# The triangular solve of a chunked recurrence: the whole triangle in two banks of PSUM, and its inverses applied as 64x64 diagonal tiles

## The chip, the cores and the metric

The kernel runs on one core of a Trainium2 chip. It has five engines with a queue each: TensorE (PE in the profile; its weight loads are PEld), VectorE (DVE), ScalarE (ACT), GpSimd (POOL) and SyncE (SP, which issues DMAs here). TensorE writes its results to PSUM, eight banks of 128 x 512 fp32 words; everything else lies in SBUF or in device memory. Each engine works its own queue in order and waits on semaphores. The metric is the device time of one launch in microseconds (us); less is better.

## The reference, cut to what matters

The kernel computes a recurrent attention (a state of 40 x 40 for each of 4 x 8 batch-heads, over 768 steps) and a mixture of experts behind it:

```python
for t in range(S):                       # S = 768, D = 40, B*H = 32
    y[:, :, t] = einsum('bhd,bhde->bhe', rt, state)
    Sa = einsum('bhde,bhe->bhd', state, at)
    state = state * wt[:, :, None, :] - einsum('bhd,bhe->bhde', Sa, bt) \
            + einsum('bhd,bhe->bhde', vt, kt)
x = y as [B*S, H*D]                      # 3072 tokens of 320
# experts: tokens with x @ w_skip > 0 go to the expert of their largest
# logit (8 experts, 320 -> 1024 -> 320, relu), scaled by the softmax weight
# of that logit, and are added to x; the others pass through.
```

All of it is fp32. What matters here is the attention. Because each step removes `Sa` (which depends on the state) and adds it back along `b`, 32 steps at once form a triangular system: with N the strictly triangular 32 x 32 matrix of products of `a` and `b` inside a chunk, the chunk needs the inverse of (1 - N), applied to what the old state and the chunk's own `k`, `v` give.

## The kernel before, in words

The 768 steps are cut into 24 chunks of 32, and `attn` walks them in one Python loop, `for c in range(NC)`. Four chunks make a group `ph` (six groups), and 64 steps make a half-group `h`. The two halves of the heads, `x` = 0 and 1, run as two interleaved recurrences. For each chunk and each `x` the path of the recurrence is: `ux` (16 matmuls against `L1`, one for each of 16 batch-heads, into PSUM, then one ScalarE copy to `UXs`), `uq` (the chunk's inverse applied to `UXs`, then four ScalarE copies into `R1t`, and a mask on POOL), `sst` (the new state, again through PSUM and ScalarE or VectorE), and for every second chunk `rs` (the state scaled back by VectorE). Beside that path run `m1` (the products that make N, one pair of calls for each `h` and `x`), `kbt` and `wtt` (transposes on TensorE), `m2` (products of `v` and `r`), `yy` (the output, one VectorE multiply `XS` for each chunk, and two DMAs out), scans on VectorE (`scan_z`, `scan_w`), products on POOL (`kbm`, `l1a`) and the routing of finished tokens to the experts (`m.route`, many small VectorE operations, and an indirect DMA).

The inverses come from `tinv(ph)`, for one group at a time, while the chunks of the group before it run. There are 128 systems (4 chunks x 32 batch-heads) and each lies in one partition, so the solve is only VectorE. It is a forward substitution by columns: step j multiplies column j of N by row j of the inverse found so far (an outer product of (31-j) x k elements, into a scratch tile `tmp_`), and subtracts that from the rows below. The columns of the inverse are split in two blocks that go side by side, so that the pair of operations of one block stands between the pair of the other. The first `SPL` = 8 columns (`X0`) lie in a PSUM bank (`px`), the other 24 columns (`Xi`) in SBUF, in the big tile `M`. In the profile the first block's operations read `M<-M,px` (product) and `px<-px,M` (subtraction). Those of the second block read `M<-M` for both. 30 steps in the first block and 22 in the second make 104 VectorE operations for each of the five solves (groups 1 to 5; group 0 has a solve of its own, `tinv0`). At the end ScalarE copies `X0` to `Xi`, and one VectorE transpose writes the inverses to `TB`, where `uq` reads them as weights: four matmuls of 32 x 32 for each `hh`, one for each block of 32 partitions.

Two things set the order of the work. The first two chunks and the last two stand in the order in which the code calls them. From chunk 2 up to chunk 22 the calls are only recorded by `Rec`, which then places them (`flush`, `plan`): a list scheduler with estimated costs for each operation, which decides the order on all five engines and which bank of PSUM each tile gets. In the profile the recorded instructions carry L209 and the others L109. The planner may use the banks of `pq`, `pc` and `ps`, two of each, so six; `py` (one bank, for `yy`) and `px` (one bank, for `X0`) are not its own. Outside the plan `m1`, `kbt`, `wtt`, `m2`, `s1`, `s2` and the routing take their tiles from the ring `ps_p`, which from the end of the prologue on is the two banks `pq`. The planner is told which POOL and VectorE operations depend on each other, but its costs know nothing of one engine slowing another.

## Time and profile before

| | us |
|---|---|
| median of three runs | 662.9 (660.15 to 670.07) |
| the profiled execution | 660.01 |
| its span in the profile | 658.2 |
| VectorE busy | 519.6 (79%) |
| TensorE busy | 507.4 (77%) |
| ScalarE busy | 423.6 (64%) |
| POOL busy | 321.6 (49%) |

The span is cut into stages below: the prologue and chunk 0 (0 to 89 us), chunk 1 (to 110.2), chunks 2 and 3 (to 152.2), then four chunks in each of the next stages (to 231.2, 311.6, 391.8 and 454.6), the end of the recurrence and the last routing (to about 507), and the experts (to 658). A row of the groups' view gives line, engine, operation, tiles written and read, one shape, the count, then busy us and mean ns of one, then the idle time of the engine before them. Shapes are written partitions x elements. A row of the timeline gives start and duration in us, then engine, line, operation and tiles. A matmul of fp32 is recorded as two instructions, so 16 calls read x32.

### The profile page before, as it was taken

To read this page: it belongs to the slowest core of one execution; us is meant where nothing else is said; L and a number is where in the kernel's file an instruction comes from. 1 tells how busy PE (TensorE), PEld (TensorE's weight loads), DVE (VectorE), ACT (ScalarE), POOL (GpSimd) and SP (SyncE) were. 2 spreads that over 40 slices of the span, in tenths; PEclk is the share of its full clock that TensorE was granted. 3 is DMA by queue.
4 is the path that set the end of the run, shared out by engine and by line. 5 is a ranking of instruction groups with operands and counts; after the bars stand their busy time and mean duration, and the time that the engine had idled before them with its cause. 6 is when DMAs were issued, how large, how long until landed. Compare 5 with 4: busy or idle time off the path is not lost. (4 is left out here: it accounts for less than half of the span.)

```text
span 658.2 us, 30327 instructions
## 1 busy us (share of the span) xinstructions
PE 507.4 (77%) x13236; PEld 424.8 (65%) x13236; DVE 519.6 (79%) x1182; ACT 423.6 (64%) x1103; POOL 321.6 (49%) x256
## 2 busy tenths in 40 slices
PE   5766676687588778858758578888678799999994
PEld 2544465566476657637547466767566599899994
DVE  7998778988989789997998977884274458888871
ACT  6463565587766867757768578898966155455540
POOL 5491952645536665375733634333131156566661
PEclk9697778779877986888969799999977799999998
DMA  7784566352444525345334243454535166667200
GB/s 183 215 229 153 133 181 218 114 150 86 124 119 132 162 74 142 107 130 161 102 106 121 82 129 101 133 168 119 156 99 146 57 193 207 214 216 233 81 25 24
DMA packets 67817, 90.85 MB, mean 138 GB/s; under 512 B 32756, under 2 KB 54849, under 8 KB 66190
## 3 DMA queue, kind: packets, MB, share of 16 engines
q1 hardware_dynamic: 62638, 74.31, 39.0%
q0 software_dynamic: 5040, 14.54, 6.8%
q8 instruction: 106, 1.74, 1.1%
q14 instruction: 33, 0.27, 0.1%
HBM read 74.03 MB, written 17.08 MB: 138 GB/s over the span
## 5 line engine op out<-in xcount | busy, mean ns | idle before, releaser
L209 DVE TENSOR_TENSOR M<-M 128x130 f32<-128x130 f32 (+10 forms) x202 | 106.2, 526 | 2.2
L209 ACT COPY R1t<-pq 32x416 f32<-32x416 f32 (+4 forms) x218 | 84.1, 386 | 31.7 <-PE pq L209 28.7
L209 POOL TENSOR_TENSOR R1t<-R1t,mc 64x512 f32<-64x512 f32 x40 | 53.8, 1346 | 86.3 <-ACT R1t L209 62.8
L109 POOL TENSOR_TENSOR WL<-WR,WH 128x1280 fp32r<-128x1280 f32 (+1 forms) x21 | 57.6, 2779 | 8.7 <-ACT WH L109 8.6
L209 ACT COPY R1t<-pc 32x128 f32<-32x128 f32 (+4 forms) x146 | 53.3, 365 | 9.7 <-PE pc L209 7.7
L209 PE MATMUL py<-L2t,R1t 128*32 128x40 f32 x1280 | 22.9, 220 | 27.4 <-DVE XS L209 14.4
L209 POOL TENSOR_TENSOR WR<-WR,M 128x1024 f32<-128x1024 f32 x14 | 33.7, 2422 | 14.9 <-DMA WR<-kb 14.6
L109 ACT CAST WH<-WR 128x1024 fp32r<-128x1024 f32 (+1 forms) x35 | 39.6, 1132 | 0.0
L209 DVE TENSOR_TENSOR px<-px,M 128x168 f32<-128x168 f32 (+8 forms) x141 | 37.1, 263 | 3.1
L209 PEld LDWEIGHTS py<-L2t,R1t 128*32 128x32 f32 x1280 | 18.1, 124 | 31.9 <-issue 16.9
L109 DVE CAST ti<-xe 128x2 int32<-128x2 f32 x8 | 38.0, 4747 | 0.2
L109 POOL DMA_INDIRECT out<-ro,ti x16 | 15.7, 982 | 45.7 <-PE pq L109 21.8
L109 ACT ACTIVATE hH<-pc 128x512 fp32r<-128x512 f32 x21 | 12.6, 598 | 38.3 <-PE pc L109 38.3
L209 POOL DMA_INDIRECT xg<-XS,ix x20 | 24.6, 1232 | 25.1 <-DVE M L209 11.1
L209 DVE TENSOR_TENSOR M<-M,px 128x168 f32<-128x168 f32 (+8 forms) x141 | 34.7, 246 | 1.3
L209 DVE TENSOR_TENSOR_SCAN M<-M 128x1041 f32<-128x1041 f32 (+1 forms) x14 | 32.5, 2320 | 0.2
L209 POOL TENSOR_TENSOR M<-M,mc 128x256 f32<-128x256 f32 x16 | 12.1, 756 | 41.6 <-issue 25.4
L109 PE MATMUL pc<-xH,WH 128*128 128x256 f32 x126 | 32.4, 282 | 0.0
L109 DVE TENSOR_TENSOR WL<-WR,WH 128x1024 fp32r<-128x1024 f32 (+1 forms) x19 | 23.8, 1253 | 8.4 <-ACT WH L109 7.8
L209 DVE TENSOR_TENSOR R1t<-pc,D 40x512 f32<-40x512 f32 (+1 forms) x32 | 19.2, 601 | 13.3 <-PE pc L209 12.9
L209 PE MATMUL ps<-R1t,L2t 128*40 128x40 f32 (+1 forms) x512 | 26.3, 244 | 2.5 <-ACT R1t L209 1.1
L209 PE MATMUL pq<-UX,TB 32*32 32x72 f32 (+1 forms) x800 | 23.6, 262 | 5.5 <-ACT R1t L209 5.3
(380 smaller groups left out, 1692.9 us busy)
## 6 DMA issues: line engine op xcount, KB each, us to landing
WR<-kb SPq DMA_DIRECT2D x10, 1024.0 KB
WR<-w SPq DMA_DIRECT2D x16, 640.0 KB
WR<-w SPq DMA_DIRECT2D x16, 512.0 KB
vvt<-vv POOLq DMA_DIRECT2D x21, 256.0 KB, 4.1
rrt<-rr POOLq DMA_DIRECT2D x10, 512.0 KB, 5.6
M<-wt SPq DMA_DIRECT2D x9, 520.5 KB
M<-at SPq DMA_DIRECT2D x8, 512.0 KB
WR<-w SPq DMA_DIRECT2D x16, 256.0 KB
```

What stands on the lines that cost most here:

```text
L109: if not s.on: return fn(*a,**k)
L209: for fn,a,k,own in s.tasks[i].calls: fn(*[at(x,own) for x in a],**{n:at(x,own) for n,x in k.items()})
```

## The change

It does three things.

The second block of the solve moves from SBUF to PSUM. `SPL` becomes 12, so that the first block is 32 x 12 words (`X0`) and the rest of the triangle is 20 x 20 (`X1`), each in a bank of its own, and no operation of the solve proper has all its operands in SBUF any more. The second block now has 18 steps instead of 22, and a tile `X1` of 400 words is copied back by ScalarE beside `X0`.

The banks are dealt out anew: `px` gets two banks and `pq` one. The planner so has five banks instead of six, and the ring `ps_p` has one bank where the order is that of the code.

`uq` applies the inverses from chunk 4 on as 64 x 64 weights, with two 32 x 32 blocks on the diagonal and zeros beside them: two matmuls for each `hh` instead of four. For that the last transpose of the solve writes to `NL_` (in `M`), and eight DMAs on SP's queue set the blocks into three tiles `TBw`, two in `SCR` and one in `TB`, which three DMAs from a tensor of zeros have cleared (issued at chunks 2 and 5). The first group keeps the 32 x 32 form.

```diff
--- before.py
+++ after.py
@@ -221,7 +221,7 @@
         if len(shape)==2: return t
         ax=["abcd"[q] for q in range(len(shape)-1)]
         return t.rearrange("p ("+" ".join(ax)+") -> p "+" ".join(ax),**{a:v for a,v in zip(ax,shape[1:])})
-G2=1; TD=(1,3); BU0=6; BU=(2,0,0,0); BX=(0,0,0,0,0,1,0,0,0,0,2,2,1,1,1,0,0,0,1,2,0,1,1,1,1,0,1,0,0); SPL=8; SCAN_POOL=0; RN=192; RB=((),()); RLAST=(('0c','1b','3a','3c'),('0a','0c')); P2=0
+G2=1; TD=(1,3); BU0=6; BU=(2,0,0,0); BX=(0,0,0,0,0,1,0,0,0,0,2,2,1,1,1,0,0,0,1,2,0,1,1,1,1,0,1,0,0); SPL=12; SCAN_POOL=0; RN=192; RB=((),()); RLAST=(('0c','1b','3a','3c'),('0a','0c')); P2=0
 ROUTE=('0c',('0c','1b','3c'),('0c','1b','3c'))
 WT=(1,0,0,0,1)
 def attn(ctx,tc,i,m,out,X):
@@ -232,7 +232,7 @@
     cp=P("const",1).pool; wk=P("wk",1); wk2=P("wk2",2); wk3=P("wk3",3); wk4=P("wk4",4)
     pp=m.pp
     bk=lambda n,k: [pp.tile([128,512],F32,name=f"{n}{q}") for q in range(k)]
-    PQ,PC,PS,PY,PX=bk("pq",2),bk("pc",2),bk("ps",2),bk("py",1),bk("px",1)
+    PQ,PC,PS,PY,PX=bk("pq",1),bk("pc",2),bk("ps",2),bk("py",1),bk("px",2)
     rec.banks={t.name:t for t in PQ+PC+PS}; rec.rest=[t.name for t in PS]
     ps_c,ps_s,ps_p=(Ring(t,rec) for t in (PC,PS,PQ)); ps_y,ps_x=Ring(PY),Ring(PX); m.ps=ps_p
     V,A,G,TE,SP=nc.vector,nc.scalar,nc.gpsimd,nc.tensor,nc.sync
@@ -241,19 +241,22 @@
     NR1=2; NL=4; NL2=2; NTB=3
     mQ,idn=m.mQ,m.idn
     WR=m.WR
-    mp=tc.tile_pool(name="M",bufs=1,side="right"); M=mp.__enter__().tile([128,13300],F32,name="M")
+    mp=tc.tile_pool(name="M",bufs=1,side="right"); M=mp.__enter__().tile([128,13400],F32,name="M")
     off=[0]
     def mv(n):
         o=off[0]; off[0]+=n; return M[:,o:o+n]
     w_,Z_,rv,a_,AB_,NL_,X_,l3=(mv(n) for n in (1041,1042,1041,1024,1024,1024,1024,1024))
-    AT_=[mv(256) for _ in range(2)]; Wx_=[mv(1040).rearrange("p (a b) -> p a b",a=16) for _ in range(4)]; tmp_=[mv(192) for _ in range(2)]; an=[0]
+    AT_=[mv(256) for _ in range(2)]; Wx_=[mv(1040).rearrange("p (a b) -> p a b",a=16) for _ in range(4)]; tmp_=[mv(240) for _ in range(2)]; an=[0]
     sq=lambda t: t.rearrange("p (a b) -> p a b",a=32)
     KBa=[WR[:,2048*q:2048*q+2048].rearrange("p (u c q t) -> p u c q t",u=16,c=2,q=2) for q in range(4)]
     L1t=cp.tile([128,4096],F32,name="L1t")
     l1s=[[WR[:,8192:9216],WR[:,9216:10240],WR[:,10240:11264]]+[l3]+[L1t[:,1024*q:1024*q+1024] for q in range(4)]][0]
     L1=[[l1s[2*n+x].rearrange("p (u c t) -> p u c t",u=16,c=2) for n in range(NL)] for x in range(2)]
     TB=cp.tile([128,NTB*512],F32,name="TB"); SCR=cp.tile([128,2048],F32,name="SCR")
-    TBa=[TB[:,512*q:512*q+512].rearrange("p (h m) -> p h m",h=16) for q in range(NTB)]
+    TBn=[TB[:,o:o+512].rearrange("p (h m) -> p h m",h=16) for o in (1024,0)]
+    TBw=[t.rearrange("p (h m) -> p h m",h=16) for t in (SCR[:,0:1024],SCR[:,1024:2048],TB[:,0:1024])]
+    TBa=TBn
+    def tbw(h): return TBw[(h+1)%NTB]
     L2t=cp.tile([128,5120],F32,name="L2t"); R1t=cp.tile([128,5632],F32,name="R1t")
     L2=[[L2t[:,1280*(2*n+x):1280*(2*n+x)+1280].rearrange("p (c u d) -> p c u d",c=2,u=16) for n in range(NL2)] for x in range(2)]
     R1=[[R1t[:,3328*n+(1664,1152)[n]*x:][:,:(1664,1152)[n]].rearrange("p (u n) -> p u n",u=16) for n in range(NR1)] for x in range(2)]
@@ -391,28 +394,29 @@
         ab=AB[0]
         NLt=sq(NL_)
         V.transpose(NLt.rearrange("p a b -> p (a b)"),ab.rearrange("p a b -> p (a b)"))
-        Xi=sq(X_)
-        X0=ps_x.tile([128,32,SPL],F32)
+        Xi=sq(X_); K=32-SPL
+        X0=ps_x.tile([128,32,SPL],F32); X1=ps_x.tile([128,K,K],F32)
         V.tensor_tensor(X0,NLt[:,0:SPL].rearrange("p s t -> p t s"),m.mT[:,:,0:SPL],ALU.mult)
-        V.tensor_tensor(Xi[:,:,SPL:32],NLt[:,SPL:32].rearrange("p s t -> p t s"),m.mT[:,:,SPL:32],ALU.mult)
+        V.tensor_tensor(X1,NLt[:,SPL:32,SPL:32].rearrange("p s t -> p t s"),m.mT[:,SPL:32,SPL:32],ALU.mult)
         V.memset(X0.rearrange("p a b -> p (a b)")[:,0:SPL*SPL:SPL+1],-1.0)
-        V.memset(Xi.rearrange("p a b -> p (a b)")[:,33*SPL::33],-1.0)
+        V.memset(X1.rearrange("p a b -> p (a b)")[:,::K+1],-1.0)
         yield
         for i in range(1,31):
             q=[]
-            for g,(j,lo,hi,X) in enumerate(((i,0,min(i,SPL),X0),(i+SPL,SPL,i+SPL,Xi))):
+            for g,(j,o,X) in enumerate(((i,0,X0),(i+SPL,SPL,X1))):
                 if j>30: continue
-                n=31-j; k=hi-lo
-                tmp=tmp_[g]
-                tv=tmp[:,:n*k].rearrange("p (a b) -> p a b",b=k)
-                V.tensor_tensor(tv,NLt[:,j,j+1:32].unsqueeze(2).broadcast_to([128,n,k]),X[:,j,lo:hi].unsqueeze(1).broadcast_to([128,n,k]),ALU.mult)
-                q.append((tv,X[:,j+1:32,lo:hi]))
+                n=31-j; k=min(i,SPL) if g==0 else i
+                tv=tmp_[g][:,:n*k].rearrange("p (a b) -> p a b",b=k)
+                V.tensor_tensor(tv,NLt[:,j,j+1:32].unsqueeze(2).broadcast_to([128,n,k]),X[:,j-o,0:k].unsqueeze(1).broadcast_to([128,n,k]),ALU.mult)
+                q.append((tv,X[:,j+1-o:32-o,0:k]))
             for tv,xv in q: V.tensor_tensor(xv,xv,tv,ALU.subtract)
             yield
-        A.copy(Xi[:,:,0:SPL],X0)
-        s0=(2*ph)%NTB; s1=(2*ph+1)%NTB
-        t0=TBa[s0]; d=bass.AP(t0.tensor,t0.offset,(tuple(t0.ap[0]),(TBa[s1].offset-t0.offset,2),(32,16),(1,32)))
-        V.transpose(d.rearrange("p h (x f) m -> p m x h f",x=2),Xi)
+        A.copy(Xi[:,:,0:SPL],X0); A.copy(Xi[:,SPL:32,SPL:32],X1)
+        t0=NL_.rearrange("p (w h m) -> p w h m",w=2,h=16)
+        V.transpose(t0.rearrange("p w (x f) m -> p m x w f",x=2),Xi)
+        for w in range(2):
+            for b in range(4):
+                r=slice(32*b,32*b+32); SP.dma_start(tbw(2*ph+w)[r,:,32*(b%2):32*(b%2)+32],t0[r,w])
         yield
     def tinv0(Xi):
 
@@ -484,11 +488,11 @@
         UXd[x]=UXs
     def uq(c,x):
         if c<0: return
-        R=R1[x][c%NR1]; Tb=TBa[(c//2)%NTB]; uu=slice(uo[x],uo[x]+32); n=RW[c%2]
+        R=R1[x][c%NR1]; uu=slice(uo[x],uo[x]+32); n=RW[c%2]; k=32 if c<4 else 64; Tb=TBn[c//2] if c<4 else tbw(c//2)
         UQ=ps_c.tile([128,4,n],F32,tag="pc",name="psUQ")
         for hh in range(4):
-            for b in range(4):
-                q=slice(32*b,32*b+32)
+            for b in range(128//k):
+                q=slice(k*b,k*b+k)
                 TE.matmul(UQ[q,hh,:],Tb[q,x*8+hh*2+c%2,:],UXd[x][q,hh,0:n],start=True,stop=True)
         for b in range(4):
             A.copy(R[uu,4*b:4*b+4,:],UQ[32*b:32*b+32,:,:])
@@ -720,7 +724,10 @@
             if c: rs(c,1)
             else: warm(BX[8])
             if c==1: s2(1,0,(0,0,1,1))
-            if c==2: s2(1,1,(0,0,1,1))
+            if c==2:
+                s2(1,1,(0,0,1,1))
+                for q in range(2): SP.dma_start(SCR[:,1024*q:1024*q+1024],i['zer'][:,0:1024])
+            if c==5: SP.dma_start(TB[:,0:1024],i['zer'][:,0:1024])
             T()
             if j==1: kbt(2*ph+1,2)
             if j==3: kbt(2*ph+2,2)
@@ -764,7 +771,7 @@
         next(ra)
         yy(NC-1,1)
         run_all(ra)
-        m.pr=[Ring.of(ps_c.t+ps_x.t),Ring.of(ps_s.t+ps_y.t),ps_p]
+        m.pr=[Ring.of(PC+PX[:1]),Ring.of(PS+PX[1:]),Ring.of(PQ+PY)]
         p2=[m.pr[0].tile([128,512],F32) for _ in range(2)]; pt=[p2[0][:,0:256],p2[0][:,256:512],p2[1][:,0:256]]
         rb=m.route(xl[:,1:2],1,NC-1,lambda: onehot(1))
         warm(WT[1]); m.xacc(pt,0)
```

On VectorE, where the solve of the third group (`ph` = 2) begins, the order before is:

```order
L209 STREAM_TRANSPOSE M<-M 128x1024
L209 TENSOR_TENSOR px_106<-M,mc 128x256
L209 TENSOR_TENSOR M<-M,mc 128x32x24
L209 TENSOR_TENSOR M<-M,px_106 128x30
L209 TENSOR_TENSOR px_106<-px_106,M 128x30
L209 TENSOR_TENSOR M<-M,px_106 128x58
L209 TENSOR_TENSOR px_106<-px_106,M 128x29x2
L209 TENSOR_TENSOR M<-M 128x22
L209 TENSOR_TENSOR M<-M,px_106 128x84
L209 TENSOR_TENSOR M<-M 128x22
```

The same place in the changed program, with operations of the recurrence (`R1t`) between:

```order
L209 STREAM_TRANSPOSE M<-M 128x1024
L209 TENSOR_TENSOR px_105<-M,mc 128x384
L209 TENSOR_TENSOR R1t<-ps_102,D_511 40x8x40 x2
L209 TENSOR_TENSOR px_106<-M,mc 128x400
L209 MEMSET px_105 128x12
L209 MEMSET px_106 128x20
L209 TENSOR_TENSOR M<-M,px_105 128x30
L209 TENSOR_TENSOR M<-M,px_106 128x18
L209 TENSOR_TENSOR px_105<-px_105,M 128x30
L209 TENSOR_TENSOR px_106<-px_106,M 128x18
```

Each operation of the second block now names a bank, `px_106`, and the triangle's mask is applied into two banks (384 and 400 elements) instead of one bank and `M` (256 and 768).

On TensorE, in chunk 1, where the tiles come from the ring in the order of the code, the order before is (`WR,L1t` are the two calls of `m1`, `mc,WE` is `wtt`, `mc,WR` is `kbt`):

```order
L109 MATMUL pq_99<-WR,L1t 32x64 x16
L109 MATMUL pq_100<-WR,L1t 32x64 x16
L109 MATMUL pq_99<-mc,WE_456 128x104 x4
L109 MATMUL pq_100<-mc,WR 128x104 x4
L109 MATMUL ps_103<-mc 128x512
```

and in the changed program:

```order
L109 MATMUL pq_99<-WR,L1t 32x64 x32
L109 MATMUL pq_99<-mc,WE_456 128x104 x4
L109 MATMUL pq_99<-mc,WR 128x104 x4
L109 MATMUL ps_102<-mc 128x512
```

The four tiles that went to two banks in turn now go to one bank, one behind the other.

On SP, where the inverses of the group `ph` = 3 are set in place in the changed program (`R1t<-vt` is `load_v`, `WR<-M` the DMAs of `m1`), with nothing of the kind before:

```order
L209 DMA WR<-M 32x256 x4
L209 DMA WR<-zer 32x1024
L209 DMA R1t<-vt 32x16x40
L209 DMA SCR<-M 32x16x32 x4
L209 DMA TB<-M 32x16x32 x4
L209 DMA M<-zer 32x1024
L209 DMA WR<-M 32x256 x4
L209 DMA M<-at 128x1024
```

Eight DMAs stand on SP's queue ahead of the next loads.

## The prediction

> **What bounds the kernel now.** The page's chain of waits reaches back only to 506 us, into the expert phase, which this change leaves alone. So I read the recurrence by stages. The timeline of TensorE gives the first matmul with new inverses (`uq` of chunks 4, 8, 12, 16 and 20), and so the stages' bounds:
>
> ```profile
> 152.17 0.92 PE L209 MATMUL pq<-UX,TB 32*32 32x104 f32 x32
> 231.21 0.92 PE L209 MATMUL pq<-UX,TB 32*32 32x104 f32 x32
> 311.58 1.11 PE L209 MATMUL pq<-UX,TB 32*32 32x104 f32 x32
> 391.80 0.92 PE L209 MATMUL pc<-UX,TB 32*32 32x104 f32 x32
> 454.59 1.28 PE L209 MATMUL pc<-UX,TB 32*32 32x104 f32 x32
> ```
>
> Busy time by stage (from:to, length; then busy us of PE, PEld, DVE, ACT and POOL with instruction counts; granted clock, DMA share, GB/s):
>
> ```profile
> 89.00:110.20 21.20, 14.77 (x527) 12.38 (x524) 17.27 (x65) 14.92 (x42) 5.25 (x4) 0.83 0.68 203
> 110.20:152.20 42.00, 31.23 (x1089) 26.75 (x1087) 36.56 (x92) 28.06 (x81) 21.27 (x22) 0.80 0.38 115
> 152.20:231.20 79.00, 58.87 (x1986) 48.32 (x1980) 71.50 (x185) 58.27 (x168) 42.14 (x38) 0.85 0.43 125
> 231.20:311.60 80.40, 60.07 (x1995) 50.34 (x1984) 71.54 (x185) 58.48 (x168) 45.55 (x38) 0.81 0.42 124
> 311.60:391.80 80.20, 55.18 (x1983) 45.68 (x1977) 73.48 (x180) 56.24 (x162) 41.94 (x34) 0.87 0.39 110
> 391.80:454.60 62.80, 52.68 (x1860) 42.66 (x1853) 47.56 (x177) 55.51 (x159) 21.39 (x22) 0.97 0.46 130
> ```
>
> In the three stages of about 80 us DVE is busy 89 to 92%, ACT and PE some 70 to 75%. The fourth runs the same recurrence and the same kind of solve in 62.8 us, with POOL at 21 instead of 42 us. So VectorE sets the pace from 152 to 392, and the groups of its time say why. First all solves, then the second block (`M<-M`) in each of the four stages:
>
> ```profile
> L209 DVE TENSOR_TENSOR M<-M 128x130 f32<-128x130 f32 (+10 forms) x202 | 106.2, 526 | 2.2
> L109 DVE TENSOR_TENSOR M<-M 128x42 f32<-128x42 f32 (+7 forms) x16 | 5.6, 353 | 0.0
> ...
> L209 DVE TENSOR_TENSOR M<-M 128x22 f32<-128x22 f32 (+10 forms) x44 | 26.7, 607 | 0.5
> ...
> L209 DVE TENSOR_TENSOR M<-M 128x22 f32<-128x22 f32 (+10 forms) x44 | 26.4, 600 | 0.5
> ...
> L209 DVE TENSOR_TENSOR M<-M 128x22 f32<-128x22 f32 (+10 forms) x44 | 28.6, 651 | 0.5
> ...
> L209 DVE TENSOR_TENSOR M<-M 128x22 f32<-128x22 f32 (+10 forms) x44 | 14.4, 328 | 0.4
> ```
>
> The same 44 operations take 26 to 29 us where POOL works much, and 14.4 where it works little. The timelines of DVE and POOL show it happen:
>
> ```profile
> 205.71 2.20 DVE L209 TENSOR_TENSOR M<-M 128x42 f32<-128x42 f32 x1
> 208.15 0.23 DVE L209 TENSOR_TENSOR px<-px,M 128x56 f32<-128x56 f32 x1
> 208.28 3.08 DVE L209 TENSOR_TENSOR M<-M 128x22 f32<-128x22 f32 x1
> ...
> 205.69 2.15 POOL L209 TENSOR_TENSOR WR<-WR,M 128x1024 f32<-128x1024 f32 x1
> 209.17 2.15 POOL L209 TENSOR_TENSOR WR<-WR,M 128x1024 f32<-128x1024 f32 x1
> ```
>
> A product of 42 elements begins with a POOL operation (205.69 to 207.84) and ends with it at 207.91. The one of 22 ends at 211.36, with the POOL operation that ends at 211.32. Between them an operation with a bank of PSUM among its operands took 0.23 us. VectorE's operations with all operands in SBUF wait for POOL's; those with PSUM don't.
>
> **The solve on VectorE.** The second block's 18 steps do sum i(19-i) = 1140 elements, each in a product and a subtraction. Prices come from the shapes of the first block:
>
> ```profile
> L209 DVE TENSOR_TENSOR px<-px,M 128x184 f32<-128x184 f32 x4 | 1.4, 354 | 0.1
> L209 DVE TENSOR_TENSOR px<-px,M 128x8 f32<-128x8 f32 x5 | 0.9, 174 | 0.2
> L209 DVE TENSOR_TENSOR M<-M,px 128x184 f32<-128x184 f32 x4 | 1.4, 344 | 0.1
> L209 DVE TENSOR_TENSOR M<-M,px 128x8 f32<-128x8 f32 x5 | 0.8, 163 | 0.2
> L109 DVE TENSOR_TENSOR M<-M 128x60 f32<-128x60 f32 x2 | 0.4, 212 | 0.0
> ...
> L209 DVE TENSOR_TENSOR M<-M,mc 128x768 f32<-128x768 f32 x4 | 6.0, 1498 | 0.0
> ...
> L209 DVE TENSOR_TENSOR px<-M,mc 128x256 f32<-128x256 f32 x4 | 3.3, 827 | 0.1
> ```
>
> That is 166 ns + 1.02 an element for a subtraction, 155 + 1.03 for a product. 18 x 0.321 + 1140 x 0.00205 = 8.1 us a solve. The first block grows from 8 to 12 columns, so by 2024 - 1140 = 884 elements (2024 is the old second block): 884 x 0.00205 = 1.8 us. Masks: 0.83 + 1.50 before; two of about 1.0 by the same rows (1.31 ns an element between them) after, so 0.3 less. The last transpose I leave at its 2.0. A solve loses its second block and gains 9.9 - 0.3 = 9.6: the four stages lose 17.1, 16.8, 19.0 and 4.8 us of DVE. The first solve had 106.2 + 5.6 - 26.7 - 26.4 - 28.6 - 14.4 = 15.7 and loses 6.1.
>
> The Trainium skill (VectorE: DVE Perf Modes, "The TRN2 errata") speaks against this. It gives an operation from PSUM a fixed 120 cycles and one from SBUF 58, at 0.96 GHz, so an estimate by that page makes each of the 36 operations of the second block 65 ns dearer than in SBUF, 2.3 us a solve. No such price shows here: `M<-M` of 60 elements, undisturbed in the fifth row, took 212 ns, and the two lines above give 217 and 227 for 60. The sum stays with the rows.
>
> **What is late next.** With 17 us less, DVE would be at 55 of 80 us. The stage from 391.8 shows how full others can be when VectorE doesn't bind: ACT 55.51/62.8 = 88%, PE 52.68/62.8 = 84%. ACT gains a copy of 400 elements and 128 more in the other one:
>
> ```profile
> L209 ACT COPY R1t<-pq 32x416 f32<-32x416 f32 x52 | 25.8, 496 | 5.9 <-PE pq L209 5.2
> ```
>
> About 0.5 + 0.1 us a solve. So the stages come out at the longer of PE/0.84 and (ACT + 0.6)/0.88: 70.1, 71.5 and 65.7 us, all by PE (ACT gives 66.9, 67.1, 64.6). Against 79.0, 80.4 and 80.2 that is 8.9 + 8.9 + 14.5 = 32 us. The fourth is already there: 0. Of the first solve most lies from 110.2 to 152.2 (DVE 87%); PE/0.84 gives 37.2, so at most 5 us, and I take 4.
>
> **The 64x64 tiles.** How long is `uq`?
>
> ```profile
> 217.80 0.79 PE L209 MATMUL ps<-R1t,L2t 128*40 128x40 f32 x32
> ...
> 219.01 0.70 PE L209 MATMUL pq<-UX,TB 32*32 32x72 f32 x32
> ...
> L209 PE MATMUL py<-L2t,R1t 128*32 128x40 f32 x1280 | 22.9, 220 | 27.4 <-DVE XS L209 14.4
> ```
>
> A single matmul's 220 ns is, by my estimate, all fill and drain. What is left of the 0.70, with four blocks at once and so 8 deep, is 0.48/8 = 60 ns for 72 columns, 0.83 ns a column. The row above, 40 wide and so two at once, is 16 deep: 0.57/16 = 36 ns for 40 columns, 0.89. Half the instructions, two at once, are again 8 deep: 0.7 us as before. The bounds are 0 and half of it for 40 `uq`, 14 us. I take 0.
>
> **The new DMAs** stand between the solve and its use. SP's own pace, a POOL-queue load's time to landing (the nearest row with one), and two last transposes:
>
> ```profile
> 217.69 2.62 SPq L209 DMA_DIRECT2D L1t<-M  x4
> ...
> vvt<-vv POOLq DMA_DIRECT2D x21, 256.0 KB, 4.1
> ...
> 220.32 1.98 DVE L209 STREAM_TRANSPOSE TB<-M 128x1024 f32<-128x1024 f32 x1
> ...
> 383.61 1.98 DVE L209 STREAM_TRANSPOSE TB<-M 128x1024 f32<-128x1024 f32 x1
> ```
>
> The first chunk needs four of the eight: 2.6 us to issue and up to 4.1 to land, 6.7. Between transpose and first use lay 231.21 - 222.30 = 8.9 us, and 391.80 - 385.59 = 6.2. A faster solve ends earlier, so I count 0; without that cover it is up to 5 x 6.7 = 34 us. The 5.2 us in which SP issues all eight delay the loads behind them (`at`, `v` of a later chunk, N's products), which are a chunk ahead, some 16 to 20 us. The 1.5 MB of zeros hide beside a DMA share of 0.4.
>
> **The lost bank.** In chunk 1 thirteen tiles now share one bank. `m1` is the worst, because VectorE and ACT both empty it:
>
> ```profile
> 83.71 0.76 DVE L109 STREAM_TRANSPOSE M<-pq 128x128 f32<-128x128 f32 x2 [6.19 <-POOL WR L109]
> ...
> 83.74 0.38 ACT L109 COPY M<-pq 128x128 f32<-128x128 f32 x1
> ```
>
> 0.76 us for each of two pairs, and as much for two or three transposes that stand next to each other: +3 us (0 to 13 x 0.8 = 10). The last two chunks' routing is one chain anyway: +1. In the plan five banks do the work of six. Four chunks need 74 tiles (`ux` 8, `uq` 8, `m2` 8, `rs` 4, `sst` 16, `m1` 8, `kbt` 8, `wtt` 4, routing 10). A tile of `uq` is held at least 0.92 + 4 x 0.50 = 2.9 us; six banks always full would be 6 x 80/74 = 6.5. The middle, 4.7, is 74 x 4.7/5 = 70 us a stage on five banks: as long as PE's, so banks don't yet rule, but there is no room left. I add 1 us for each of five solves, +5.
>
> **Sum**, on the profiled execution's 660.0: -32 - 4 + 3 + 1 + 5 = -27, 633. The median shown is 2.9 above that execution, so 636.
>
> **The rivals.** *All engines pack better*: PE goes above 84% (the expert stage shows it near 100%) and ACT rules. Stages of 66.9, 67.1, 64.6 give -41; -5 for the first solve, +4, no bank price: 618 for the execution, 621 median. With `uq` a little shorter, 610. For it speaks that PE's 84% is only what one stage happened to reach, against it the lost bank. 0.22.
>
> *The banks give the gain back.* Held 5.0 us, the stages take 74 and the sum is -18 - 4 + 4, about 645 median; at 5.4 us they take 80 and nothing is left, 663. The part of this within 2% of before gets 0.19.
>
> *Slower.* The same mechanism from 5.7 us on: 74 x 5.7/5 = 84.4, +14 over three stages, +3 in the fourth (58 tiles, as `m1` and `kbt` are absent: 66), and +4 at both ends: above 676. At 6 us it is near 700. It decides if tiles wait for their emptying nearly as long as six full banks would let them; against it, VectorE will empty them sooner. 0.07.
>
> *The stalls do not go*, since scans and `l1a` still meet POOL: but they are there now too, and only the `M<-M` group is counted above.
>
> **How the numbers follow.** The forecast case, 624 to 649, has 0.52. Faster by over 2% (below 649.6; 2% is about what a measurement of this kernel can tell) is it and the better packing: 0.74. Within 2%: 0.19. Slower (above 676): 0.07. The range 610 to 656 leaves out the slower case, the worse half of the banks' case and a few hundredths below.
>
> **What would show it.** Right: no `M<-M` group of tensor products of 22 to 132 elements; `px<-px,M` at 0.17 to 0.40 us whatever POOL does; DVE near 55 us in a stage of about 70, with PE first at 84% or more. Wrong: stages still near 80 us with PE and ACT waiting for each other's tiles (banks), or `uq` of a group's first chunk waiting for a DMA (the block transfer), or chunk 1 longer by far more than 3 us.

## The result

| | before | after |
|---|---|---|
| median of 17 runs each | 661.67 us (656.13 to 670.07) | 668.12 us (662.76 to 672.71) |
| the profiled execution | 660.01 | 672.71 |
| its span | 658.2 | 670.9 |

The ratio of the times is 1.0099, with a 95% interval of 1.0072 to 1.0126. The change makes the kernel 1% slower, where the forecast was 636 us, 4% faster. The profiled execution of after lies 4.6 us above its median, that of before 1.7 below, so stage lengths of the two differ by a little more than the kernels do.

The page of the changed kernel gives the engines' busy time first:

```profile
PE 517.6 (77%) x12596; PEld 430.0 (64%) x12596; DVE 464.9 (69%) x1142; ACT 428.6 (64%) x1108; POOL 320.7 (48%) x256
```

VectorE lost 519.6 - 464.9 = 54.7 us of work, and the time went up all the same. The timeline of TensorE shows the first `uq` of chunks 4, 8, 12, 16 and 20, so the bounds of the same stages (start, duration, then what ran):

```profile
159.39 0.93 PE L209 MATMUL pc<-UX,SCR 64*64 64x104 f32 x16
...
244.28 0.93 PE L209 MATMUL pc<-UX,TB 64*64 64x104 f32 x16
...
323.61 0.93 PE L209 MATMUL pq<-UX,SCR 64*64 64x104 f32 x16
...
401.61 1.00 PE L209 MATMUL pc<-UX,SCR 64*64 64x104 f32 x16 [2.54 <-DVE R1t L209]
...
467.43 0.93 PE L209 MATMUL pq<-UX,TB 64*64 64x104 f32 x16
```

Busy time in these stages, from chunk 1 on (from:to, length, then PE, PEld, DVE, ACT, POOL):

```profile
92.80:120.10 27.30, 18.14 (x563) 15.39 (x556) 18.36 (x69) 15.92 (x45) 8.85 (x6) 0.75 0.56 166
120.10:159.40 39.30, 29.32 (x1118) 23.82 (x1116) 31.16 (x81) 29.81 (x84) 18.31 (x21) 0.91 0.54 143
159.40:244.30 84.90, 61.53 (x1894) 51.16 (x1886) 55.84 (x169) 59.44 (x168) 43.35 (x38) 0.82 0.46 131
244.30:323.60 79.30, 61.73 (x1853) 51.31 (x1852) 59.63 (x177) 59.33 (x168) 44.84 (x38) 0.81 0.48 134
323.60:401.60 78.00, 57.30 (x1863) 47.10 (x1859) 58.05 (x180) 58.98 (x166) 42.96 (x35) 0.89 0.42 116
401.60:467.40 65.80, 51.53 (x1620) 42.81 (x1620) 39.18 (x159) 53.02 (x153) 19.51 (x20) 0.90 0.52 139
```

In the three stages that were 89 to 92% VectorE, that engine is now busy 66, 75 and 74% of the time, and they take 84.9, 79.3 and 78.0 us against 79.0, 80.4 and 80.2. No engine is above 78% in them. Chunk 1 takes 27.3 us instead of 21.2.

The solve itself became what it was meant to be. No tensor product of the form `M<-M` is left among VectorE's groups of the plan (L209); only group 0's own solve in the prologue still has some. The two groups of the solve are short (line, engine, operation, tiles, shape, count, then busy us and mean ns):

```profile
L209 DVE TENSOR_TENSOR px<-px,M 128x210 f32<-128x210 f32 (+11 forms) x222 | 53.6, 268 | 1.9
L209 DVE TENSOR_TENSOR M<-M,px 128x210 f32<-128x210 f32 (+11 forms) x222 | 50.8, 257 | 1.8
```

The timelines of VectorE and POOL show a product of the second block (34 elements) inside two POOL operations that follow each other:

```profile
248.66 0.18 DVE L209 TENSOR_TENSOR M<-M,px 128x34 f32<-128x34 f32 x1
...
246.33 4.29 POOL L209 TENSOR_TENSOR WR<-WR,M 128x1024 f32<-128x1024 f32 x2 [8.17 <-DMA WR<-kb]
```

It takes 0.18 us, although POOL is at work from 246.33 to 250.62. So the question is not whether the stalls went, but why 55 us less on the fullest engine is worth so little, and what made the rest slower.

### The profile page after: what moved, and what is told of

Its sections match the earlier page's. It is cut to its first block, busy times and chain, and to the rows that moved or that the text cites. A ratio compares the mean times of both kernels' runs of the same rounds, so it can differ in the third digit from the quotient of the medians.

```text
span 670.9 us, 29096 instructions
## 1 busy us (share of the span) xinstructions
PE 517.6 (77%) x12596; PEld 430.0 (64%) x12596; DVE 464.9 (69%) x1142; ACT 428.6 (64%) x1108; POOL 320.7 (48%) x256
## 4 chain that ended last, share of the span: by engine, by line
PE 34%; DVE 21%; ACT 16%; issue 11%; DMA 8%; POOL 5%; POOLq 0%; SPq 0%; DVEq 0%; ACTq 0%
PE pc L209 7%; PE pc L109 7%; ACT R1t L209 7%; PE ps L109 7%; DVE M L209 6%; PE px L109 5%; PE ps L209 3%; DVE M L109 3%; DMA xg<-XS,ix 3%; DVE R1t L209 3%; DVE px L209 3%; ACT L2t L209 2%; PE pq L209 2%; PE pq L109 2%; DVE ti L109 2%
## 5 line engine op out<-in xcount | busy, mean ns | idle before, releaser
L209 ACT COPY R1t<-pc 32x128 f32<-32x128 f32 (+4 forms) x236 | 89.1, 377 | 26.1 <-PE pc L209 20.8
L209 POOL TENSOR_TENSOR R1t<-R1t,mc 64x512 f32<-64x512 f32 x40 | 54.3, 1358 | 71.0 <-ACT R1t L209 50.9
L209 DVE TENSOR_TENSOR R1t<-pc,D 40x512 f32<-40x512 f32 (+1 forms) x56 | 34.1, 610 | 39.9 <-PE pc L209 38.8
L209 POOL TENSOR_TENSOR WR<-WR,M 128x1024 f32<-128x1024 f32 x14 | 32.1, 2315 | 48.0 <-DMA WR<-kb 20.9
L209 DVE TENSOR_TENSOR px<-px,M 128x210 f32<-128x210 f32 (+11 forms) x222 | 53.6, 268 | 1.9
L209 DVE TENSOR_TENSOR M<-M,px 128x210 f32<-128x210 f32 (+11 forms) x222 | 50.8, 257 | 1.8
L209 POOL DMA_INDIRECT xg<-XS,ix x20 | 27.8, 1391 | 38.3 <-DVE ix L209 9.4
L209 PE MATMUL py<-L2t,R1t 128*32 128x40 f32 x1280 | 23.1, 222 | 23.9 <-POOL R1t L209 17.1
L209 ACT COPY R1t<-pq 32x288 f32<-32x288 f32 (+4 forms) x92 | 35.9, 390 | 7.3 <-PE pq L209 5.9
L209 DVE TENSOR_TENSOR_SCAN M<-M 128x1041 f32<-128x1041 f32 (+1 forms) x14 | 37.5, 2678 | 0.5
L209 PEld LDWEIGHTS py<-L2t,R1t 128*32 128x32 f32 x1280 | 18.1, 125 | 29.2 <-POOL R1t L209 20.7
L209 ACT COPY R1t<-ps 40x288 f32<-40x288 f32 (+3 forms) x72 | 26.9, 373 | 11.4 <-PE ps L209 10.3
L109 PE MATMUL ps<-mc 128*128 128x512 f32 x36 | 25.5, 817 | 4.8 <-DMA mc<-mc 3.7
L109 PE MATMUL ps<-WH,hH 128*128 128x320 f32 x88 | 27.6, 314 | 0.0
L109 PE MATMUL pc<-xH,WL 128*128 128x256 f32 x126 | 27.2, 281 | 0.0
```

What stands on the lines that cost most here:

```text
L109: if not s.on: return fn(*a,**k)
L209: for fn,a,k,own in s.tasks[i].calls: fn(*[at(x,own) for x in a],**{n:at(x,own) for n,x in k.items()})
```

## The experiments

Ratios are to the kernel before on the same chip, with 95% intervals; medians are in us. Stage lengths come from each kernel's own profiled execution, cut at the same `uq` as above. Of an edit the main line is shown; `...` stands for lines left out. Some kernels leave work out so that their numbers are wrong; where it matters, the kernel's flag for its slow fallback is also held down in them.

### One part at a time

**Five banks alone.** In the kernel before, the planner gets five banks, while the ring of the code's order keeps its two.

```diff
-    rec.banks={t.name:t for t in PQ+PC+PS}
+    rec.banks={t.name:t for t in PQ[:1]+PC+PS}
...
```

> The kernel before with one edit: the planner (chunks 2 to 21) may use five banks of PSUM instead of six. The first and last two chunks keep the ring of two banks. Theory 'banks' (VectorE's relief is real, the sixth bank was worth about as much): slower than before by 20 to 40 us, 680 to 700. Theory 'path' (VectorE did not set the pace, so neither the relief nor the bank matters much; what sets it is the chain through all the engines in their fixed order): within 6 us of before, 656 to 668.

661.64, ratio 0.9984 (0.9926 to 1.0042). In this kernel the sixth bank is worth nothing that can be measured. The stages are 80.2, 81.1, 74.9 and 66.2 us.

**No second block at all.** The steps of the second block are left out, so 24 of the 32 columns of each inverse aren't solved, and nothing else changes.

```diff
-                if j>30: continue
+                if j>30 or g: continue
```

> The kernel before, six banks, with the second block of each solve left out: the 220 operations M<-M (111.8 us of VectorE) are not done, and the second block keeps only its masked start, so the inverses are not the reference's. Theory 'banks' (or any in which VectorE set the pace): the stages of four chunks fall from 80 to about 66 us, 35 to 50 us in all, 612 to 627. Theory 'path': under 12 us, 650 or more.

629.89, ratio 0.954 (0.9492 to 0.9589), 31 us less, between the two expected ranges. These operations held VectorE for 106.2 + 5.6 = 111.8 us before. But VectorE's busy time fell only from 519.6 to 448.0, by 71.6 us, because operations that stayed took longer. Its windows for the three full stages and the fourth:

```profile
144.50:218.50 74.00, 58.33 (x1987) 47.43 (x1980) 55.96 (x141) 58.09 (x167) 44.00 (x39) 0.88 0.46 135
218.50:290.10 71.60, 57.62 (x1991) 47.56 (x1980) 51.43 (x141) 58.05 (x167) 42.60 (x38) 0.88 0.48 139
290.10:363.30 73.20, 57.39 (x1990) 46.82 (x1977) 56.34 (x142) 55.72 (x160) 42.34 (x34) 0.91 0.43 121
363.30:429.10 65.80, 52.16 (x1863) 42.67 (x1858) 41.32 (x127) 55.17 (x159) 21.41 (x22) 0.96 0.44 125
```

This is the prediction's limit put to the test. By PE/0.84 these stages would take 69.4, 68.6 and 68.3 us; they take 74.0, 71.6 and 73.2, with every engine at 81% or less. VectorE is busy 51 to 56 us in them, the level that the forecast expected (55), and for it the forecast had 70.1, 71.5 and 65.7. The fourth stage, where VectorE lost 6 us too, is not shorter at all: 65.8 against 62.8.

**Without the 64x64 tiles.** The changed kernel, with `uq` and the last transpose of the kernel before and no block DMAs and zeros.

```diff
-                r=slice(32*b,32*b+32); SP.dma_start(tbw(2*ph+w)[r,:,32*(b%2):32*(b%2)+32],t0[r,w])
+        V.transpose(d.rearrange("p h (x f) m -> p m x h f",x=2),Xi)
...
```

> The changed kernel with its 64x64 tiles undone: inverses by VectorE's transpose straight into TB, applied as 32x32, no new DMAs. Solve in two banks, five banks for the plan, ring of one. If the block transfer and its 40 DMAs cost something, this is faster than the changed kernel (668) by that, 5 to 15 us; theories 'banks' and 'path' both expect it within 4 us of the changed kernel, 664 to 672.

654.83, ratio 0.9919 (0.9874 to 0.9965): 12 to 13 us better than the whole change.

**The 64x64 tiles alone**, in the kernel before.

```diff
+                r=slice(32*b,32*b+32); SP.dma_start(tbw(2*ph+w)[r,:,32*(b%2):32*(b%2)+32],t0[r,w])
...
```

> The kernel before with the 64x64 tiles alone: eight DMAs for each solve and half the matmuls of uq, with the second block of the solve still in SBUF and six banks. If the transfer costs, 5 to 15 us slower than before; if half the instructions of uq are worth something on the path, up to 10 us faster; by the prediction's working 0, within 4 us of 662.

668.41, ratio 1.0162 (1.0086 to 1.0237). From both sides the tiles cost 1.6 to 1.8%, 11 to 13 us. The matmuls aren't the reason, since `uq` takes as long as before (0.93 us for 104 columns above, against 0.92). SP's queue is a suspect. In the changed kernel, after the transpose that ends a solve, it does this (the first row is VectorE's, the SPq rows are issues):

```profile
217.83 1.98 DVE L209 STREAM_TRANSPOSE M<-M 128x1024 f32<-128x1024 f32 x1
...
223.07 2.68 SPq L209 DMA_DIRECT2D TB<-M  x4
225.79 3.43 SPq L209 DMA_DIRECT2D SCR<-M  x4
...
234.91 0.43 SPq L209 DMA_DIRECT2D M<-at  x1
...
240.00 0.53 SPq L209 DMA_DIRECT2D WR<-kb  x1
```

The eight issues hold the queue for 6.2 us, and the load of `kb` for the next half-group comes 20.2 us behind the transpose's end. Before, that end was at 222.30 and `kb` went out 2.5 us later:

```profile
224.82 0.53 SPq L209 DMA_DIRECT2D WR<-kb  x1
```

The waits of POOL's `kbm` for that load between 100 and 460 us (total us, times, longest) are, before, with the tiles alone, and after the whole change:

```profile
POOL WR L209 <- DMA WR<-kb: 14.6, 3, 6.9
```

```profile
POOL WR L209 <- DMA WR<-kb: 25.6, 3, 10.9
```

```profile
POOL WR L209 <- DMA WR<-kb: 20.9, 3, 8.2
```

### The queue of the block DMAs

The planner counts an issue on SP as 0.06 us, and the rows above show about 0.6 to 0.85. So it packs issues that it thinks are free, whatever stands behind them. The next kernels give it a truer number, in the changed kernel and, as a control, in the one before:

```diff
-            return (0.06 if e=='S' else 1.0 if 'ind' in op else 0.6),2.0+by/2.6e5
+            return (0.62 if e=='S' else 1.0 if 'ind' in op else 0.6),2.0+by/2.6e5
```

> The changed kernel, 64x64 tiles and all, with one number of the planner mended: it counts 0.62 us for each DMA that SP issues, which is what the traces show, instead of 0.06. Theory 'queue' (the eight DMAs of a solve hold SP for some 6 us that the plan doesn't know of, and the loads behind them come late): much of the transfer's cost goes, 653 to 660 instead of 668. Theory 'lottery' (any edit deals the order of the plan anew, and that alone moves the time by some us either way): anywhere from 655 to 675. A theory in which the transfer itself is late: 665 or more.

> Control: the kernel before with the same number mended (0.62 instead of 0.06 us for an issue on SP). Theory 'queue': it has no burst of eight, so within 4 us of before, 657 to 665. Theory 'lottery': up to 8 us either way.

The changed kernel comes down to 661.05, ratio 0.9997 (0.9954 to 1.004), 7 us less, just outside the range of theory 'queue' and inside that of 'lottery'. The kernel before gets no better: 663.65, ratio 1.011 (1.006 to 1.016). That fits a price that helps only where the eight DMAs are, but it doesn't show it: the control moved as far the other way, and another order alone moves the time by 0.7% (below). And what the price mended isn't the wait for `kb`, which is longer here than in the changed kernel:

```profile
POOL WR L209 <- DMA WR<-kb: 26.0, 4, 11.6
```

So late `kb` loads show that the order has moved. They don't show what the tiles cost.

**Another queue.** The same DMAs, issued by POOL, whose issues the planner prices at 0.6.

```diff
-                r=slice(32*b,32*b+32); SP.dma_start(tbw(2*ph+w)[r,:,32*(b%2):32*(b%2)+32],t0[r,w])
+                r=slice(32*b,32*b+32); G.dma_start(tbw(2*ph+w)[r,:,32*(b%2):32*(b%2)+32],t0[r,w])
```

> The changed kernel with the eight block DMAs of each solve issued from POOL's queue instead of SP's; bytes, packets, tiles and matmuls are the same, and the planner prices a POOL issue at 0.6 us. Theory (SP's queue is held): kb, at and wt are issued again within some 3 us of the solve's end, as before; POOL's wait for kb goes from 20.9 us back to near the 14.6 of the kernel before, the stage from 152 on goes from 85 to about 79 us, and the median from 668 to 655 to 660 (with the blocks left out it was 654.8). POOL pays about 5 x 5 us of issues, of which it has room. Rival (the price is the transfer itself, its 21,500 more packets, or the zeros, and not the queue): the loads are issued early but land late, and it stays at 665 to 672. A second rival (what the plan makes of eight more short tasks, whatever queue they are on): the stage from 152 on stays at 85 to 88 us though kb is issued early and is not waited for.

664.77, ratio 1.0017 (0.9974 to 1.006): 3 to 5 us better than with SP, and 6 to 10 short of the kernel without tiles. None of the three expectations is met in full. Its timeline shows why this isn't the clean test it was meant to be:

```profile
217.02 1.95 DVE L209 STREAM_TRANSPOSE M<-M 128x1024 f32<-128x1024 f32 x1
...
231.98 2.48 SPq L209 DMA_DIRECT2D L1t<-M  x4
234.56 0.53 SPq L209 DMA_DIRECT2D WR<-kb  x1
```

`kb` is still issued 15.6 us behind the solve, though SP has no block to issue: the plan puts it behind the DMAs of N's products. POOL waits for it as long as after the whole change, nearly:

```profile
POOL WR L209 <- DMA WR<-kb: 18.7, 4, 8.5
```

The lateness of this load therefore isn't the queue's occupation alone; it is also where the plan puts it once the tiles are there. The stage that begins with chunk 4 is 79.6 us here, but chunks 2 and 3 take 50.7 instead of 39.3, and both kernels reach chunk 20 at about the same time (466.4 and 467.4 us). So the loss has changed place. Pricing the issues truly or moving them to another queue gives back 3 to 7 of the 11 to 13 us, hardly more than another order can. What the rest is, transfers or order, these runs don't settle.

### The ring of one bank

**One bank for the code's order, in the kernel before**; the planner keeps six.

```diff
-            ps_p=pq
+            ps_p=Ring(PQ[:1],rec)
```

> The kernel before with one bank instead of two in the ring of the first two and the last two chunks (the plan keeps its six). By the stages of the solve-only kernel (chunk 0 longer by 2.5 us, chunk 1 by 2.9): slower by 3 to 7 us, 664 to 668. If the ring costs nothing, within 2 us of before.

669.42 (658.9 to 674.03, four runs, too wide for a ratio). Chunk 1 takes 21.6 us in its profile, against 21.2, and the chunk before it 31.2 against 29.5. The median is 7 us up and this profile doesn't show where, so this run decides nothing.

**A second bank where one lies idle.** The kernel without tiles, whose ring also uses a bank of `px` while the solve doesn't need it.

```diff
-            ps_p=pq
+            ps_p=Ring.of(PQ+PX[1:])
...
-                ps_p=m.ps=Ring(PQ)
+                ps_p=m.ps=Ring(PQ+PX[:1])
...
```

> The solve in two banks, without the 64x64 tiles, and with a second bank for the ring where the second bank of the solve is idle (chunk 0 and the first part of chunk 1, and after the plan). The solve-only kernel with one bank took 655; by the ring's price of 3 to 7 us this should take 648 to 652, and so beat before and the changed kernel.

651.06, ratio 0.9831 (0.974 to 0.9922), against 654.83 without this edit; chunks 0 to 3 take 96.6 us instead of 99.2 (92.6 in the kernel before). It is the fastest complete kernel of the study, 1.7% faster than before. Its windows for the three full stages and the fourth:

```profile
157.10:232.90 75.80, 55.78 (x1980) 45.45 (x1982) 59.06 (x179) 58.55 (x166) 44.59 (x39) 0.89 0.42 127
232.90:311.90 79.00, 57.93 (x1983) 47.07 (x1981) 57.31 (x174) 58.54 (x168) 45.97 (x39) 0.87 0.43 126
311.90:385.90 74.00, 55.62 (x1979) 45.60 (x1979) 51.44 (x177) 56.13 (x162) 38.74 (x33) 0.91 0.39 119
385.90:449.00 63.10, 50.40 (x1762) 40.44 (x1755) 40.27 (x160) 54.81 (x157) 20.49 (x21) 0.97 0.46 129
```

Here too VectorE is at the forecast's level, 51 to 59 us, and the stages stay at 74 to 79.

> The changed kernel, 64x64 tiles and all, with SP's true cost in the plan and the second bank for the ring as in the kernel before this one. With SP's cost alone it took 661; the ring gives 3 to 7 us back: 654 to 658. If the ring's price was only another order of the plan, 659 to 663.

The whole change with the SP price and the ring's second bank: 658.72, ratio 0.9942 (0.9894 to 0.9989), between the two expected ranges. The two repairs together take 1.6% off the change.

> The fastest kernel so far (solve in two banks, no 64x64 tiles, second bank for the ring, 651) with SP's true cost in the plan. It has no burst of eight DMAs, so theory 'queue' expects within 4 us of it, 647 to 655; 'lottery' up to 8 us either way.

The kernel without tiles, with the second bank and the SP price: 653.9, ratio 0.9876 (0.9808 to 0.9944). As in the kernel before, the price gives nothing that can be measured where there are no blocks.

**Both blocks in one bank.** The kernel before, with the new solve, both blocks overlaid in the one bank of `px`, so that six banks stay for the plan. The inverses it solves are not used further: every group is given those of the first.

```diff
+        Xb=ps_x.tile([128,512],F32); X0=Xb[:,0:32*SPL].rearrange('p (a b) -> p a b',b=SPL); X1=Xb[:,0:K*K].rearrange('p (a b) -> p a b',b=K); Xc=sq(SCR[:,0:1024])
...
```

> The solve's second block in PSUM with six banks left to the plan and two to the ring: both blocks lie over each other in the one bank of before (so the solve's numbers are wrong, and the inverses of group 0 are applied everywhere instead; all operations have the changed kernel's shapes). No 64x64 tiles. Theory 'banks' (once VectorE is freed, the sixth bank counts): at least 6 us below the kernel with five banks and the mended ring, so under 643. Theory 'path': within 5 us of it, and by 0.28 us for each of the 62 us of VectorE some 17 us below before, 642 to 650.

653.44, ratio 0.9851 (0.9748 to 0.9953), above the ranges of both theories. With six banks the new solve is worth as much as with five: about 10 us, not 36.

### How much is only order

> The kernel before with one constant of the planner moved (LET 0.8 instead of 1.0), which changes no operation, only their order. Theory 'lottery': 4 to 10 us away from before, either way. If orders of the same planner are about equally good: within 3 us, 658 to 664.

The kernel before with one number of the planner's search changed (`LET` 1.0 to 0.8), which alters the order and no work: 666.59, ratio 1.0069 (1.003 to 1.0108). Two plans of the same work lie 0.7% apart. Single differences below 1% in this study can't be told from another order.

### What paces a stage

If VectorE isn't the pace, some other engine may be. Each of the next kernels takes work from one engine.

**ScalarE:** `wchk`, sums of squares of the decays which the recurrence doesn't wait for, 14.6 us of ACT, left out from half-group 4 on.

```diff
-        if h>=NH: return
+        if h>=4: return
```

> The kernel before without the check of w on ScalarE from the fifth half-group on (wchk: two Square operations with a sum for each, 16 of them, 14.6 us of ScalarE in the recurrence at 0.72 + 0.19 us; it feeds only a safety flag, and nothing waits for it). It tells what a microsecond of ScalarE is worth. Theory 'path' (no engine sets the pace alone; VectorE's 112 us were worth 31, so 0.28 each): 2 to 6 us faster. If ScalarE is the true bound: 10 us or more. If it is idle time: 0 to 1.

661.18, ratio 1.0021 (0.9967 to 1.0074): worth nothing, where 'path' expected 2 to 6 us.

**POOL:** `l1a`, the products with N's second factor, left out from chunk 2 on (37 us of POOL); and the same with the second block left out too.

```diff
-        if h>=NH: return
+        if h>=NH or rec.on: return
```

> The kernel before with the products l1a left out from chunk 2 on (15 operations on POOL, 37.0 us; the left factor of N then holds older numbers, so the result isn't the reference's). POOL loses 37 us, and VectorE's SBUF operations have less to wait for. Theory 'path' (each engine's time counts a little because each hop of the recurrence queues behind other work on its engine): 5 to 15 us faster. If POOL sets the pace of the 80 us stages: 20 us or more. If POOL's time counts nothing: within 4 us.

> Both left out: the second block of the solve (without it alone 630) and POOL's products l1a. If POOL set the pace once VectorE is free: 615 or less. Theory 'path': 620 to 627. If POOL counts nothing: 627 to 632.

Alone 640.58, ratio 0.9673 (0.9602 to 0.9743). Without the second block as well 632.58, ratio 0.958 (0.95 to 0.966), no better than the 0.954 without the second block and with `l1a`. The 22 us alone are what was expected if POOL sets the pace, but then the second kernel should have gained too. So those 37 us of POOL were not the pace either. They held VectorE up: without them its busy time is 479.3 us, 40.3 less, and nearly all of that is the second block, which took 106.2 us before:

```profile
L209 DVE TENSOR_TENSOR M<-M 128x130 f32<-128x130 f32 (+10 forms) x202 | 69.7, 345 | 1.9
```

Once the operations that they met are gone, they cost nothing that these intervals can show.

**TensorE and ScalarE:** `kbt`, 20 us of PE and 41 us of ACT, left out from chunk 2 on; and the same with the second block left out too.

> The kernel before with the transposes kbt left out from chunk 2 on (36 tiles: 20 us of TensorE and 144 copies, 41 us of ScalarE; the factors of the state's update then hold older numbers). If ScalarE or TensorE set the pace: 20 to 35 us faster. Theory 'path': 5 to 12 us, about what the same time of VectorE was worth (112 us for 31). If their time counts nothing: within 4 us.

> The kernel before with two things left out: the second block of the solve (VectorE, 112 us of its busy time, worth 31 us by itself) and kbt from chunk 2 on (some 20 us of PE and 41 us of ACT, worth 24 us by itself). Theory (no engine paces alone; each operation taken away shortens the waits of the others, and the worth of two on different engines adds): 600 to 612. Rival (a chain of hops through the recurrence sets a floor that both removals already reach, as for l1a on POOL, whose worth was gone once the second block was): 625 to 632.

Alone 637.72, ratio 0.9671 (0.9601 to 0.9741), which lies in the range expected if ScalarE or TensorE set the pace, not in that of 'path'. It isn't a clean removal of engine time, however: TensorE's busy time fell by 8.2 us only (507.4 to 499.2) and ScalarE's by 43.4, and the state's update no longer waits for these copies. Both 614.3, ratio 0.9248 (0.9189 to 0.9307), just above the range of its theory. If the two worths simply add, the ratio is 0.954 + 0.9671 - 1 = 0.9211, which lies within the interval; a floor at 72 us a stage would have left it near 0.954. Its windows:

```profile
149.60:217.80 68.20, 52.69 (x1956) 44.16 (x1950) 52.72 (x141) 49.38 (x135) 41.46 (x38) 0.90 0.51 145
217.80:290.20 72.40, 55.34 (x1960) 46.39 (x1956) 50.84 (x141) 49.59 (x135) 42.15 (x38) 0.83 0.50 138
290.20:355.60 65.40, 49.86 (x1952) 41.00 (x1948) 50.91 (x144) 46.50 (x128) 37.57 (x32) 0.95 0.49 132
```

With work gone from three engines, no engine is above 78% in any of them, so a stage has no single engine that is full. (The middle one, at 72.4 us, is no shorter than the 71.6 without the second block alone.) Work taken from VectorE and from PE with ACT each buys a part of its own length, and they add; work on ACT alone bought nothing. But VectorE's busy time doesn't tell the worth: 40.3 us less of it bought 22 us without `l1a`, 71.6 less bought 31 without the second block, and 64.5 less (519.6 to 455.1) bought 11 with the new solve and the ring's second bank. No run shows why these differ; the order, the ring and what each kernel no longer waits for differ with them. The granted clock differs too (0.882 before, 0.869 after, 0.901 without the second block), but the kernel without `kbt` is 3% faster in a profile at 0.861, so it doesn't decide these results. My reading is that each step of the recurrence goes through PE, ACT, DVE and POOL in turn and queues on each behind other work, so that shorter queues anywhere on that path help a little. The waits of the changed kernel in its first two full stages fit that, since they are spread over many pairs of engines (us in total, times, longest):

```profile
DVE R1t L209 <- PE pc L209: 19.0, 6, 5.8
POOL WR L209 <- DMA WR<-kb: 12.9, 2, 8.2
DVE XS L209 <- PE py L209: 12.7, 3, 10.5
ACT R1t L209 <- PE pc L209: 11.7, 12, 3.2
...
PEld pc L209 <- ACT R1t L209: 9.8, 15, 1.4
POOL R1t L209 <- ACT R1t L209: 9.4, 3, 5.0
```

VectorE itself now waits 19 us for `pc` tiles of TensorE in 164 us. But what holds a stage at its length is argued here and not shown: no run changed the recurrence's own chain by itself.

## Why the prediction was wrong, point by point

**What is late next: the step that failed.** The prediction said that "VectorE sets the pace from 152 to 392", and let a relieved stage shrink to PE/0.84 or ACT/0.88, ceilings read from the one stage that was short. For this it counted 32 of its 36 us. VectorE came down as forecast, and the stages didn't follow. Without the second block it is busy 51 to 56 us in the three full stages, and the four stages together are 17.8 us shorter (302.4 to 284.6). With the new solve, no tiles and a second bank for the ring it is busy 51 to 59 us, and they are 10.5 us shorter (to 291.9). In the whole kernel the two were worth 31 us (0.954) and 11 us (0.9831).

Two things were overlooked. The first is argued, not shown: the busy share of 90% had waiting in it, and time in which an engine waits for a lock costs the kernel only where something urgent stands behind it, while the solve's results are needed only in the next stage. The second is in the traces: the fourth stage is short by work that it hasn't got, most of `m1` (71 matmul instructions in the profile against 256 in each of the others) and half of POOL's, and its granted clock was 0.97 against 0.81 to 0.87. Leaving the second block out didn't shorten it. So its ratio of PE to length is no ceiling for the others. (`kbt`, which the prediction took to be absent there, is there in full.)

**The mechanism of the stalls: right.** The second block's operations of 18 to 90 elements now take 0.17 to 0.25 us in the mean, and DVE came to 55.84 us in the first full stage, where 55 was forecast; only the 70 us around it didn't come. Over the kernel 54.7 us of VectorE's time went, and 66.0 in the kernel without tiles (519.6 to 453.6), where the terms of the five solves make 63.8. Other operations took longer meanwhile. The scans, which the prediction dismissed with "they are there now too", took this much before (first row) and after (second row):

```profile
L209 DVE TENSOR_TENSOR_SCAN M<-M 128x1041 f32<-128x1041 f32 (+1 forms) x14 | 32.5, 2320 | 0.2
```

```profile
L209 DVE TENSOR_TENSOR_SCAN M<-M 128x1041 f32<-128x1041 f32 (+1 forms) x14 | 37.5, 2678 | 0.5
```

In the kernel without tiles they take 38.1 us. So that rival had a true core: stalls don't only go, some find another victim.

**PSUM's price: right.** By the prediction's prices the products and subtractions of a new solve have a mean of 261 and 271 ns over all shapes, and the groups above have 257 and 268. So there are no 65 ns more on each operation of the second block, and the measurement stands against the rule of the Trainium skill (VectorE: DVE Perf Modes, "The TRN2 errata") that the prediction weighed.

**The 64x64 tiles: half right.** "0 for `uq`" was: 0.93 us for 104 columns, and at 72 columns 0.72 where the old form took 0.70:

```profile
192.55 0.72 PE L209 MATMUL pc<-UX,SCR 64*64 64x72 f32 x16
```

The blocks also weren't waited for by the recurrence, as forecast: the transpose shown above ends at 219.81 and the first use comes at 244.28, and no wait of TensorE between 100 and 500 us names a block DMA. The step that failed is the 0 for the new DMAs, and with it the sentence that the 5.2 us "in which SP issues all eight delay the loads behind them [...] which are a chunk ahead". It counted how early those loads are on the whole, and not where the plan puts each once the blocks are there; `kb` was 2.5 us behind a solve's end and is now 20. This term was 0 and measured 11 to 13 us, without which the sign would not have been wrong. By which way the tiles cost it, the order, the transfers or the queue, stays open.

**The banks: wrong, to the safe side.** +5 us for five banks in the plan measured nothing in the kernel before (0.9984). That alone doesn't touch the rivals that let the banks give the gain back, because they speak of stages that a relieved VectorE would let shrink; but with the new solve six banks (0.9851) are no better than five (0.9831) either, so those rivals fall. The estimate of a tile's holding time, halfway between two bounds, was no evidence that banks are short.

**The ring of one bank: in part.** Chunk 1 grew by 6.1 us where +3 stood. But it takes 21.6 us with the ring of one bank alone, 21.6 with the new solve and two banks (both blocks in one), and 24.1 with the new solve and one bank, without tiles; so it is neither alone, and why the two together cost more isn't shown. Chunks 0 to 3 take 6.6 us more in the kernel without tiles than before, and 4.0 with the second bank given back. That bank's worth in the whole kernel, 0.9%, is no more than another order can move.

**The sum.** -11 for the new solve, +11 to 13 for the tiles and some +5 for the ring make +5 to +7, and the medians differ by 6.5. This is a split of the difference more than a check of it, since the ring's term and one of the two for the tiles are differences between kernels on the same way from before to after. The rivals were about banks, packing and stalls; none said that VectorE isn't the pace, the case that came.

## What to carry to other kernels

An engine at 90% in a stage is not shown to pace it: leave its suspect work out altogether, once, and see what that is worth, and how far the engine's busy time really falls, before pricing a change that removes a part of it. Don't take a stage's ceiling from another stage that does less. Count each DMA issue on an in-order queue at its measured length, and look in the new order for which load now stands behind them, since a planner that thinks an issue free will put one in front of anything.

## What the runs showed that was not expected

The lock between VectorE and POOL doesn't go away with its largest victim. A tiny operation of 16 elements a partition with its input in SBUF (`D<-M`) was held up in none of its five instances between 150 and 400 us before, and in four of five after (one tile's instructions: least, median and most ns; then when). Before:

```profile
L209 DVE TENSOR_SCALAR D<-M x5: 168/169/171, 199.4 to 360.7; 128x16 f32<-128x16 f32 x5
```

After:

```profile
L209 DVE TENSOR_SCALAR D<-M x5: 175/2183/3081, 203.5 to 361.8; 128x16 f32<-128x16 f32 x5
```

It now often falls into an operation of POOL and ends with it, the last of the five at 363.98 us, with POOL's at 363.96:

```profile
361.80 2.18 DVE L209 TENSOR_SCALAR D<-M 128x16 f32<-128x16 f32 x1
...
359.67 4.29 POOL L209 TENSOR_TENSOR WR<-WR,M 128x1024 f32<-128x1024 f32 x2 [4.19 <-DVE M L209]
```

The Trainium skill (SBUF — State Buffer, "SBUF: two separate sides") gives the rule: VectorE and GpSimd share one pair of SBUF ports under an exclusive lock, and whichever starts first keeps it for the whole instruction; on VectorE's side this concerns operations with two inputs in SBUF and those in a mode that uses both ports. The trace agrees: the four that were held up took 1.0 to 3.1 us instead of 0.17, and each ended within 0.05 us of one of POOL's. With the longer scans above I read this as the wait being passed on to other operations in SBUF; no run singles that out.

And work on POOL can have a large worth with no wait for POOL in sight: leaving out 37 us of it saved 22 us before, and nothing that could be measured after VectorE's second block was gone. The cost was in how long VectorE's operations lasted, 36.5 us of it in the second block alone (106.2 to 69.7).
